# Reordering the head, the middle and the second token group of a fused attention and Mish-MLP kernel

## The chip, the cores and the metric

The kernel runs on one core of a Trainium2 chip. The metric is device time in microseconds (us), taken as the median of the runs shown; less is better.

## The reference

Four batches of eight heads with 768 tokens of 64 channels go through a causal attention whose scores decay with distance by a factor `lam` of each head and which has no softmax. It is computed block by block with a running state. The result, 3072 tokens of 512 channels, goes through an MLP.

```python
for b in range(S // 64):                       # blocks of 64 tokens
    intra = einsum('bhic,bhjc->bhij', qb, kb) * Dmask          # Dmask = lam ** (i - j), i >= j
    out[:, :, sl] = einsum('bhij,bhjd->bhid', intra, vb) + einsum('bhid,bhde->bhie', qb * lam_pow, kv_state)
    kv_state = lam_block * kv_state + einsum('bhsd,bhse->bhde', kb * rev_pow, vb)
x = out.transpose(0, 2, 1, 3).reshape(3072, 512)
h = x @ w_in                                   # 512 x 2048
out = (h * tanh(softplus(h))) @ w_out          # 2048 x 512
```

The matrix products run in fp16 with sums in fp32.

## The kernel before

**Tiling.** The kernel works with chunks of 128 tokens. Each of the six *groups* n = 0 to 5 holds the n-th chunk of all four batches, so 512 tokens; chunk i is group i // 4 and batch i % 4. For each group there are three kinds of work: attention, which fills `xt[n]` (the MLP's input, transposed); mm1, 16 *units* of 128 hidden columns with four matmuls of 512 tokens each into one PSUM bank `ph`, after which ScalarE writes Mish of it into `hsg`; and mm2, the product with w_out. Group 0 does mm2 plainly (`mm2_unit`, L542: 16 steps of four matmuls into a bank `po`, batches 0 and 1 first, then 2 and 3). Groups 1 to 5 do it by Strassen-like products of quarters (`fast_unit`, L685: seven steps of two blocks of eight 256-column matmuls), which need sums of weights (`weight_sum`, L559) and of tokens (`token_sum`, L572) from VectorE, named `tsum` and `gsum`.

**Order.** The schedule is written by hand: every engine executes its instructions in the order of the program. The main loop (L737) lists the units of group n and, after given units (`room`, L754 and L756), puts in *pieces* of the attention of group n + 1. PSUM has eight banks: `ph` twice, `po` twice, and `pk`, `pq`, `pS` and `pO` once each. An instruction that takes a bank waits until the reader of what was there is done.

**The head (L700 to L736).** GpSimd (POOL) issues the loads of chunks 1 to 3 of group 0, then w_in in six transfers (its first quarter in three), w_out in four, then group 1's chunks. Chunk 0's k and q come over two other queues. Without a state yet, the attention of chunk c is `first_t` (L211: PE transposes k and q into `pk` and `pq`, ScalarE and VectorE copy them out as `pkT` and `pqT`), `first_s` (L228: scores in two banks, `pS` and one `po`, and two VectorE products with the decay mask `dm`, giving `sb`) and `first_o` (L241: the product with v into `pO`, copied by ScalarE into `xt[0]`). The order on PE is t0 s0 t1 s1 o0 t2 s2 o1 t3 o2 s3, units 0 and 1 on the first 384 tokens around o3, and then mm1. `busy(m)` (L161) puts m matmuls of 512 zero columns in between. `pair_decays` (L188, two small VectorE copies and an exponential on ScalarE) stands between s0 and t1, and the exponential for `lk` and the load of the Mish table between s0 and o0.

**Group 0 to group 1.** After units 2 to 9 the kernel builds the states of group 0 in eight halves (`att_kv`, L296; `att_w`, L310). Group 1's attention is done in eight *halves* (one chunk, four heads): `att_a` (L324: transposes, the state product `pv`; on VectorE `qT` and two sums `raw`, on ScalarE two copies `kz`), `att_s` (L355: scores; VectorE's `sb`) and `att_o` (L367: output; ScalarE's `xt`). 21 of these 24 pieces stand between mm2 steps 8 to 15, and the last three between the first units of group 1.

**Group 1 and on.** The attention of group n + 1 for n of 1 and more comes as six pieces for two pairs of chunks: `pair_a` (L389: state products; VectorE's four `raw` and one `state`), `pair_s` (L408: scores and the state's part; VectorE's four `sb`), `pair_o` (L438: output; VectorE's four `xtok`, then two DMA transposes into `xt`). In group 1 they stand after units 6, 8, 10, 11, 14 and 18, counted over 16 mm1 units and 14 blocks of the fast product, and after units 2, 5, 7, 9, 12 and 16 later. `turn` (L268) scales k on VectorE or GpSimd and issues two DMA transposes on SyncE's queue (SP).

Of the kernel before, what the change touches and what calls it, by code (L numbers as in the profile page):

```python
# [20 lines left out]
def kernel(  # L21
# [12 lines left out]
    C = 128  # L34
# [49 lines left out]
    cuts = (0, 128, 256, DF // WS)  # L84
    win0 = [const.tile([128, NKC, b_ - a_], F16, name=f"win0{a_}") for a_, b_ in zip(cuts, cuts[1:])]
    win = [None] + [const.tile([128, NKC, DF // WS], F16, name=f"win{s}") for s in range(1, WS)]
    wout = [const.tile([128, NKI // WS, DMO], F16, name=f"wout{s}") for s in range(WS)]

    def load_win(s):
        w = DF // WS  # L90
        if s == 0:
            for t, a_, b_ in zip(win0, cuts, cuts[1:]):
                nc.gpsimd.dma_start(
                    out=t, in_=moe_w_in[:, a_:b_].rearrange("(k p) f -> p k f", p=128))
            return
# [61 lines left out]
    nc.vector.tensor_scalar(out=ident, in0=rel, scalar1=0.0, scalar2=None, op0=ALU.is_equal)  # L157
# [3 lines left out]
    def busy(m):  # L161

        t = ps.tile([128, 4 * C], F32, name="busy", tag="ph", bufs=2)
        for _ in range(m):
            nc.tensor.matmul(t, kzero, kzero2, start=True, stop=True)  # L165
# [13 lines left out]
    lbc = const.tile([128, JP], F32, name="lbc")  # L179
    lqt = const.tile([128, H], F32, name="lqt")  # L180

    def decays(t):
        for j in range(JP):
# [4 lines left out]
    def pair_decays():  # L188
        lnh = lnb.rearrange("p (j t) -> p j t", t=2)
        for hp in range(2):  # L190
            rs = slice(64 * hp, 64 * hp + 64)
            nc.vector.tensor_copy(lnp[rs, :], lnh[rs, :, hp])
        nc.scalar.activation(lbc, lnp, AF.Exp, scale=float(C))
# [6 lines left out]


    lbm = const.tile([128, JP, 128], F32, name="lbm")
# [8 lines left out]
    def first_t(c):  # L211

        out_ = []
        for src, name in ((k0 if c == 0 else kn[c], "pk"), (q0 if c == 0 else qn[c], "pq")):
# [7 lines left out]
            if name == "pk":  # L222
                nc.scalar.activation(out_[-1], pt, AF.Copy)
            else:
                nc.vector.tensor_copy(out_[-1], pt)
# [50 lines left out]
    wst = [[const.tile([128, 2, 128], F16, name=f"w{b}{hf}") for hf in range(2)] for b in range(B)]  # L276
# [33 lines left out]
    def att_w(s):  # L310
        n, b, hf = s.n, s.b, s.hf
        w = wst[b][hf]
        lb = lbm[:, 2 * hf : 2 * hf + 2, :]
        if n == 0:
            nc.vector.tensor_tensor(out=w, in0=s.pv, in1=lb, op=ALU.mult)
        else:
            sum_rows(n, b, s.pv, 2 * hf, 2, lambda rs: w[rs, :, rs])
# [6 lines left out]
    def att_a(s):  # L324
# [25 lines left out]
        elif hf == 0:  # L350
            turn(i + 1)
# [15 lines left out]
    def att_o(s):  # L367
# [7 lines left out]
        for p in range(2):  # L375
            j = 2 * hf + p
            nc.tensor.matmul(psO[:, p, :], wst[b][hf][:, p, :], s.qT[:, p, :],
# [101 lines left out]
    def att_pieces(n):  # L479
        halves = att_halves(n)  # L480
        out_ = []
        for t in range(len(halves) + 2):
            if t < len(halves):
                out_.append((att_a, halves[t]))
            if 0 <= t - 1 < len(halves):
                out_.append((att_s, halves[t - 1]))
            if 0 <= t - 2 < len(halves):
                out_.append((att_o, halves[t - 2]))
        return out_


# [10 lines left out]
    def mm1_part(n, ni, lo, hi):  # L502

        if lo == 0:
            ph_t[ni] = ps.tile([128, GT], F32, name="ph", tag="po" if ni == 2 and n < 2 else "ph", bufs=2)
        w = DF // WS // 128
        for kc in range(NKC):
            nc.tensor.matmul(  # L508
                ph_t[ni][:, lo:hi],
                win0[min(ni, 2)][:, kc, max(ni - 2, 0) * 128 : max(ni - 2, 0) * 128 + 128] if ni < w  # L510
                else win[ni // w][:, kc, (ni % w) * 128 : (ni % w) * 128 + 128],
# [3 lines left out]
    def mm1_unit(n, ni):  # L515
# [7 lines left out]
        mark.append(hsg[n][0:1, ni, 0:1])  # L523

# [175 lines left out]
    first_halves = att_halves(0)  # L700
    nh = len(first_halves)
# [12 lines left out]
    first_t(1)  # L714
    nc.scalar.preload_act_table(AF.Mish)
    busy(1)
    first_s(1)
    first_o(0)
    busy(3)
    first_t(2)  # L720
    busy(1)
    first_s(2)
    first_o(1)
    busy(3)
    first_t(3)
    first_o(2)
    busy(1)
    first_s(3)
    mm1_part(0, 0, 0, GT - C)
    first_o(3)  # L730
    mm1_part(0, 1, 0, GT - C)
    scale_k(0)
    nc.vector.memset(lbm, 0.0)
# [3 lines left out]
    for n in range(NG):  # L737
        units = [(mm1_unit, (n, ni)) for ni in range(NKI)]

        if n == 0:  # L740
# [114 lines left out]
```

## Time and profile before

| | |
|---|---|
| median of three runs | 206.41 us (206.38, 206.41, 208.25) |
| time of the profiled execution | 206.31 us |
| its span, first to last instruction | 204.5 us |
| PE busy | 195.3 us |
| VectorE busy | 137.8 us |
| ScalarE busy | 90.3 us |
| GpSimd busy | 82.8 us |

The 1.8 us between span and time lie around the instructions. PE's busy time holds the zero matmuls of `busy`, and a matmul's end is modelled, so busy PE is not PE at full pace. How much each stage loses is read from the chain of work and from the pace of unbroken matmuls. In the rows, PEld is the weight load of PE, DVE is VectorE, ACT is ScalarE, and L with a number is the line of the kernel.

### The profile page before, as it was taken

The numbers are of one execution on the slowest core, as the hardware profiler recorded it, in microseconds if no ns is written. First come the engines' busy times: TensorE is split into PE (matmuls) and PEld (weight loads), VectorE is DVE, ScalarE is ACT, GpSimd is POOL, SyncE is SP. The second block draws the span as 40 slices with busy tenths as digits, with TensorE's granted clock in tenths as the row PEclk, the third lists the DMA queues.
The fourth block names the chain that finished last, engine by engine and source line by source line (L and its number), as shares of the span: only waits on it lengthen the run. The fifth ranks groups of instructions, "written<-read, shape, count | busy, mean of one in ns | idle before, by whom it ended". The sixth has DMA issues, their size and how long they took to land.

```text
span 204.5 us, 4393 instructions
## 1 busy us (share of the span) xinstructions
PE 195.3 (95%) x1736; PEld 127.3 (62%) x1736; DVE 137.8 (67%) x277; ACT 90.3 (44%) x159; POOL 82.8 (40%) x128
## 2 busy tenths in 40 slices
PE   7788999999999979999999999999999999999993
PEld 2455544467655459855578855488745688544893
DVE  5857670689879996759994759995727774122543
ACT  5375668466674522045542065431156530466310
POOL 7997333899903876000898000996000000000000
PEclk9999999999999999999999999999999999999999
DMA  9999999999999999974699993999983122300014
GB/s 131 140 149 182 206 207 198 154 212 152 157 181 154 89 132 121 204 201 82 45 122 168 229 187 77 79 126 180 173 221 67 39 55 84 123 0 3 2 67 138
DMA packets 112471, 26.77 MB, mean 131 GB/s; under 512 B 102594, under 2 KB 111938, under 8 KB 112450
## 3 DMA queue, kind: packets, MB, share of 16 engines
q0 software_dynamic: 78080, 13.37, 91.8%
q1 hardware_dynamic: 31392, 10.49, 26.6%
q10 hardware_dynamic: 2978, 2.62, 4.5%
q8 instruction: 13, 0.21, 0.5%
q14 instruction: 8, 0.07, 0.1%
HBM read 27.26 MB, written 6.29 MB: 164 GB/s over the span
## 4 chain that ended last, share of the span: by engine, by line
PE 82%; DVE 9%; ACT 3%; DMA 2%; issue 1%; ACTq 0%; DVEq 0%
PE ph L508 36%; PE z L614 13%; PE x L614 9%; PE y L614 7%; PE po L531 6%; DVE raw L287 2%; DMA qn<-in_q_dram 2%; PE fin L614 2%; PE pS L419 2%; PE pO L446 2%; DVE sb L435 2%; DVE gsum L587 1%; PE pv L397 1%; PE pS L360 1%; PE pv L303 1%
## 5 line engine op out<-in xcount | busy, mean ns | idle before, releaser
L508 PE MATMUL ph<-xt,win 128*128 128x512 f16 (+2 forms) x404 | 88.7, 369 | 0.4 <-ACT hsg L522 0.2
L522 ACT ACTIVATE hsg<-ph 128x512 f16<-128x512 f32 x96 | 57.0, 597 | 66.7 <-PE ph L508 66.6
L508 PEld LDWEIGHTS <-win 128*128 128x128 f16 x404 | 37.0, 98 | 37.6 <-issue 0.6
L614 PEld LDWEIGHTS <-gsum 128*128 128x128 f16 x336 | 31.6, 98 | 3.5
L614 PEld LDWEIGHTS <-hsg 128*128 128x128 f16 x240 | 23.2, 98 | 4.4 <-issue 0.8
L498 POOL COPY paced<-hsg 1x1 f16<-1x1 f16 x27 | 7.6, 281 | 42.2 <-ACT hsg L522 42.2
L435 DVE TENSOR_TENSOR sb<-pS,maskT 128x512 f16<-128x512 f32 x32 | 19.9, 683 | 5.3 <-PE pS L419 5.2
L69 POOL DMA_DIRECT2D kn<-in_k_dram x23 | 20.6, 896 | 6.1 <-DMA wout<-in_moe_w_out_dram 1.7
L80 POOL DMA_DIRECT2D vz<-in_v_dram x24 | 21.1, 887 | 4.2 <-DMA win<-in_moe_w_in_dram 1.7
L77 POOL DMA_DIRECT2D qn<-in_q_dram x23 | 20.3, 884 | 5.5 <-DMA wout<-in_moe_w_out_dram 3.3
L587 DVE TENSOR_TENSOR gsum<-hsg 128x1024 f16<-128x1024 f16 x20 | 13.6, 685 | 10.9 <-ACT hsg L522 10.9
L614 PE MATMUL x<-wout,hsg 128*128 128x256 f16 x160 | 19.6, 273 | 0.5 <-DVE sb L435 0.5
L614 PE MATMUL z<-tsum,gsum 128*128 128x256 f16 x160 | 19.3, 273 | 0.0
L264 DVE TENSOR_TENSOR ktil<-kn,lk 128x512 f16<-128x512 f16 (+1 forms) x20 | 13.6, 686 | 6.8 <-DMA kn<-in_k_dram 6.6
L531 PE MATMUL po<-wout,hsg 128*128 128x512 f16 x64 | 15.1, 379 | 0.0
L287 DVE TENSOR_TENSOR raw<-pv,state 64x256 f32<-64x256 f32 x24 | 10.1, 420 | 6.0 <-PE pv L397 5.7
L454 DVE TENSOR_TENSOR xtok<-pO,lqt 128x256 f16<-128x256 f32 x32 | 11.3, 417 | 1.0 <-PE pO L446 0.9
L667 DVE TENSOR_TENSOR u<-z,p 128x512 f32<-128x512 f32 x5 | 3.5, 691 | 10.0 <-PE z L614 10.0
L531 PEld LDWEIGHTS <-hsg 128*128 128x128 f16 x64 | 6.0, 98 | 5.9
L614 PE MATMUL z<-tsum,hsg 128*128 128x256 f16 x80 | 9.6, 273 | 0.0
L587 DVE TENSOR_TENSOR gsum<-hsg,gsum 128x1024 f16<-128x1024 f16 x10 | 6.6, 688 | 3.8 <-PE z L614 3.8
L165 PE MATMUL busy<-kzero 128*128 128x512 f16 x18 | 7.6, 517 | 1.2 <-DVE kzero L150 1.2
(102 smaller groups left out, 213.2 us busy)
## 6 DMA issues: line engine op xcount, KB each, us to landing
out_dram<-osum SPq DMA_DIRECT2D x14, 256.0 KB, 2.4
vz<-in_v_dram POOLq DMA_DIRECT2D x24, 128.0 KB, 5.8
kn<-in_k_dram POOLq DMA_DIRECT2D x23, 128.0 KB, 5.2
qn<-in_q_dram POOLq DMA_DIRECT2D x23, 128.0 KB, 5.5
wout<-in_moe_w_out_dram POOLq DMA_DIRECT2D x4, 512.0 KB, 16.2
win<-in_moe_w_in_dram POOLq DMA_DIRECT2D x3, 512.0 KB, 9.9
out_dram<-osum ACTq DMA_DIRECT2D x5, 256.0 KB, 4.0
out_dram<-osb ACTq DMA_DIRECT2D x4, 256.0 KB, 6.3
```

The costliest lines, as they stand in the source:

```text
L69: nc.gpsimd.dma_start(out=kn[i], in_=chunk_rows(k, i))
L77: nc.gpsimd.dma_start(out=qn[i], in_=chunk_rows(q, i))
L80: nc.gpsimd.dma_start(out=vz[i % NVB][:, :, 0:D], in_=chunk_rows(v, i))
L264: (nc.gpsimd if B < i <= 2 * B else nc.vector).tensor_tensor(out=t, in0=kn[i], in1=bc(lk, 2, D), op=ALU.mult)
L287: nc.vector.tensor_tensor(out=raw[rs, b % 2, j0 : j0 + nj, :], in0=pv[rs, :, rs], in1=olds(rs), op=ALU.add)
L435: nc.vector.tensor_tensor(out=s.sb[m][t], in0=sc[m][t], in1=bc(maskT, 1, JP), op=ALU.mult)
L454: nc.vector.tensor_tensor(out=xtok[m][:, :, t, :], in0=s.pO[t][:, m], in1=bc(lt[:, :, t], 2, D), op=ALU.mult)
L508: nc.tensor.matmul(ph_t[ni][:, lo:hi], win0[min(ni, 2)][:, kc, max(ni - 2, 0) * 128 : max(ni - 2, 0) * 128 + 128] if ni < w else win[ni // ...
L522: nc.scalar.activation(hsg[n][:, ni, :], ph_t.pop(ni), AF.Mish)
L531: nc.tensor.matmul(po, hsg[n][:, ki, b * C : (b + 1) * C], wout[part][:, kk, :], start=(ki == 0), stop=(ki == NKI - 1),)
L587: nc.vector.tensor_tensor(out=gsum[n, i][:, ks, :], in0=a, in1=b, op=op)
L614: nc.tensor.matmul(t, lhs(kk, b), rhs(kk, c, c + w), start=(fresh and kk == 0 and (alone or i == 0)), stop=(kk == HK - 1), skip_group_chec ...
```

## The change

Four things change, all of them up to the end of group 1; groups 2 to 5 keep their order.

1. *Loads and head.* The first quarter of w_in is one transfer instead of three and goes behind v of chunk 1, ahead of the loads of chunks 2 and 3. The exponentials move ahead of the copy of k0, and the Mish table load to s0. `pair_decays` becomes four copies and goes between t1 and s1. The order on PE becomes t0 s0 t1 s1 o0 o1, units 0 to 3 on tokens 0 to 255, kv0 t2 s2 kv1 o2 t3, units 0 to 3 on tokens 256 to 383, s3 o3, units 0 to 3 on tokens 384 to 511, with `busy` in between. These four units are written as `mm1_duo`: two units share a bank, each with 256 tokens, and one Mish covers both. The states of group 0 are built by whole chunks (`first_kv`, `first_w`).
2. *mm2 of group 0* runs over four banks: parts 0 and 1 of all four batches, then parts 2 and 3 batch by batch. All eight weight sums stand among these steps.
3. *Attention of group 1.* 13 pieces stand after mm2 steps 10 to 15 and 11 after the first six duos of group 1.
4. *mm1 of group 1* is 16 duos: eight for tokens 0 to 255, then eight for tokens 256 to 511. The pieces of group 2's attention stand after units 12, 14, 15, 17, 19 and 22.

```diff
-    cuts = (0, 128, 256, DF // WS)
-    win0 = [const.tile([128, NKC, b_ - a_], F16, name=f"win0{a_}") for a_, b_ in zip(cuts, cuts[1:])]
-    win = [None] + [const.tile([128, NKC, DF // WS], F16, name=f"win{s}") for s in range(1, WS)]
+    win = [const.tile([128, NKC, DF // WS], F16, name=f"win{s}") for s in range(WS)]
...
-    for f, i in ((load_q, 1), (load_v, 0), (load_k, 2), (load_q, 2)):
-        f(i)
     nc.gpsimd.iota(ek, pattern=[[0, 1]], base=MID, channel_multiplier=-1,
                    allow_small_or_imprecise_dtypes=True)
-    for f, i in ((load_v, 1), (load_k, 3), (load_q, 3), (load_v, 2), (load_v, 3)):
+    for f, i in ((load_q, 1), (load_v, 0), (load_v, 1), (load_win, 0), (load_k, 2), (load_q, 2),
+                 (load_v, 2), (load_k, 3), (load_q, 3), (load_v, 3)):
         f(i)
-    for s in range(WS):
+    for s in range(1, WS):
         load_win(s)
...
     def pair_decays():
-        lnh = lnb.rearrange("p (j t) -> p j t", t=2)
-        for hp in range(2):
-            rs = slice(64 * hp, 64 * hp + 64)
-            nc.vector.tensor_copy(lnp[rs, :], lnh[rs, :, hp])
-        nc.scalar.activation(lbc, lnp, AF.Exp, scale=float(C))
+        for src, dst in ((lnb, lnp), (lbh, lbc)):
+            lnh = src.rearrange("p (j t) -> p j t", t=2)
+            for hp in range(2):
+                rs = slice(64 * hp, 64 * hp + 64)
+                nc.vector.tensor_copy(dst[rs, :], lnh[rs, :, hp])
...
+    def first_kv(c):
+
+        first_pv[c] = ps.tile([128, JP, 128], F32, name="pv", tag="po", bufs=2)
+        for j in range(JP):
+            nc.tensor.matmul(
+                first_pv[c][:, j, :].rearrange("p (a e) -> p a e", a=2),
+                ktil[c][:, 2 * j : 2 * j + 2, :].rearrange("p h c -> p (h c)"),
+                vz[c][:, 2 * j : 2 * j + 2, 0:D], start=True, stop=True,
+            )
+
+    def first_w(c):
+        nc.vector.tensor_tensor(out=wst[c], in0=first_pv[c], in1=lbm, op=ALU.mult)
...
+    def mm1_duo(n, g, lo, hi):
...
+        h = GT // 2
+        half = lo // h
+        w = DF // WS // 128
+        if (n, g, half) not in duo_t:
+            duo_t[n, g, half] = ps.tile([128, 2, h], F32, name="ph", tag="ph", bufs=2)
+        t = duo_t[n, g, half]
+        for m in range(2):
+            ni = 2 * g + m
+            for kc in range(NKC):
+                nc.tensor.matmul(
+                    t[:, m, lo - half * h : hi - half * h],
+                    win[ni // w][:, kc, (ni % w) * 128 : (ni % w) * 128 + 128],
+                    xt[n][:, kc, lo:hi], start=(kc == 0), stop=(kc == NKC - 1),
+                )
+        if hi == half * h + h:
+            nc.scalar.activation(hsg[n][:, 2 * g : 2 * g + 2, half * h : half * h + h], t, AF.Mish)
...
-            po_t[b] = ps.tile([128, DMO], F32, name="po", tag="po", bufs=2)
+            po_t[b] = ps.tile([128, DMO], F32, name="po", tag="po" if b < 2 else "ph", bufs=2)
...
+    nc.scalar.activation(lbh, lnb, AF.Exp, scale=float(C))
+    nc.scalar.activation(lk, lnb, AF.Exp, scale=ek)
     nc.scalar.activation(k0, kn[0], AF.Copy)
-    decays(0)
+    decays(0, range(JP))
+    decays(1, range(JP - 1))
     nc.vector.tensor_copy(q0, qn[0])
+    decays(1, range(JP - 1, JP))
     nc.scalar.activation(dm[:, 0], dm[:, 0], AF.Exp)
-    decays(1)
-    first_t(0)
+    busy(2, C)
+    first_t(0, between=4)
     nc.scalar.activation(dm[:, 1], dm[:, 1], AF.Exp)
+    nc.scalar.preload_act_table(AF.Mish)
     busy(1)
     first_s(0)
+    first_t(1)
     pair_decays()
-    nc.scalar.activation(lk, lnb, AF.Exp, scale=ek)
-    busy(2)
-    first_t(1)
-    nc.scalar.preload_act_table(AF.Mish)
-    busy(1)
+    busy(3)
     first_s(1)
...
     for hp in range(2):
         rs = slice(64 * hp, 64 * hp + 64)
         nc.vector.tensor_copy(lbm[rs, :, rs], bc(lbc[rs, :], 2, D))
...
+    first_o(0)
+    busy(4)
+    first_o(1)
+    scale_k(0)
+    scale_k(1)
+    mm1_duo(0, 0, 0, 2 * C)
+    mm1_duo(0, 1, 0, 2 * C)
+    first_kv(0)
+    first_t(2)
+    first_w(0)
+    busy(2, tag="pO")
+    first_s(2)
+    first_kv(1)
+    busy(3, tag="pO")
+    first_o(2)
+    first_t(3)
+    mm1_duo(0, 0, 2 * C, 3 * C)
+    mm1_duo(0, 1, 2 * C, 3 * C)
+    first_s(3)
+    first_w(1)
+    scale_k(2)
+    scale_k(3)
+    busy(4, tag="pO")
+    first_o(3)
+    mm1_duo(0, 0, 3 * C, 4 * C)
+    mm1_duo(0, 1, 3 * C, 4 * C)
...
+    pieces = [(step[w[0]], halves[int(w[1])]) for w in (
+        "a0 a1 s0 a2 s1 o0 a3 s2 o1 s3 o2 o3 a4 a5 s4 a6 s5 o4 s6 o5 a7 s7 o6 o7").split()]
+    room = {26: 1, 27: 2, 28: 3, 29: 3, 30: 2, 31: 2}
+    units = [(mm1_unit, (0, ni)) for ni in range(4, NKI)]
+    units += [(mm2_unit, (0, b, part)) for part in range(2) for b in range(B)]
+    units += [(mm2_unit, (0, b, part)) for b in range(B) for part in range(2, WS)]
+    for u, (fn, args) in enumerate(units, 4):
+        rest = fn(*args)
+        if u < 6:
+            first_kv(u - 2)
+            first_w(u - 2)
...
+        for i, s in {16: ((0, 0),), 18: ((0, 1),), 21: ((1, 0), (2, 0), (3, 0)),
+                     24: ((1, 1), (2, 1), (3, 1))}.get(u, ()):
+            weight_sum(i, s)
+        if u == 25:
+            scale_k(B)
+        attend(room.get(u, 0), "po")
+        if rest:
+            rest()
+
+    for n in range(1, NG):
+        if n == 1:
+            units = [(mm1_duo, (n, g, lo, lo + GT // 2)) for lo in (0, GT // 2) for g in range(NKI // 2)]
+            for u, m in enumerate((2, 3, 2, 1, 2, 1)):
+                fn, args = units.pop(0)
+                fn(*args)
+                attend(m, "po")
+                if u == 1:
+                    next_state(n, 0)
+                elif u == 5:
+                    next_state(n, 1)
+                if u > 2:
+                    turn((n + 1) * B + u - 3)
...
-            room = dict.fromkeys((6, 8, 10, 11, 14, 18) if n == 1 else (2, 5, 7, 9, 12, 16), 1)
+            pieces = chunk_pieces(n + 1)
+            room = dict.fromkeys((12, 14, 15, 17, 19, 22) if n == 1 else (2, 5, 7, 9, 12, 16), 1)
...
+        sums = {9: ((2, 0),), 10: ((2, 1),), NKI - 3: ((0, 0),), NKI - 2: ((1, 0),)}
+        if n == 1:
+            sums = {9: ((2, 0),), 11: ((2, 1),), NKI - 3: ((0, 0), (1, 0))}
+        sums.update({NKI - 1: ((0, 1), (1, 1)), NKI + 2: ((3, 0),), NKI + 3: ((3, 1),)})
+        for u, (fn, args) in enumerate(units, NKI + 14 - len(units)):
+            fn(*args)
...
+            for i, part in sums.get(u, ()):
+                token_sum(n, i, part)
+            if n == 1 and u == 8:
+                turn((n + 1) * B + 3)
...
+            attend(room.get(u, 0), "po" if u < NKI - 1 else "ph")
```

More of the change, by code (lines that the diff above doesn't have):

```diff
@@ L179, with decays @@
     lbc = const.tile([128, JP], F32, name="lbc")
+    lbh = const.tile([128, H], F32, name="lbh")
     lqt = const.tile([128, H], F32, name="lqt")
[L182 to L183 removed]
+    def decays(t, js):
+        for j in js:
             nc.vector.scalar_tensor_tensor(
@@ L222, in first_t @@
             if name == "pk":
+                if between:
+                    busy(between, C)
                 nc.scalar.activation(out_[-1], pt, AF.Copy)
@@ new lines, with attend @@
+    mm1_duo(0, 0, 0, 2 * C)
[19 more added lines that the diff above has]
+    mm1_duo(0, 1, 3 * C, 4 * C)
+    def attend(m, spare):
+        for _ in range(m):
+            f2, s = pieces.pop(0)
+            s.spare = spare
+            f2(s)
@@ new lines @@
+    for n in range(1, NG):
[11 more added lines that the diff above has]
+                    turn((n + 1) * B + u - 3)
+            while ahead:
+                ahead.pop(0)()
+        else:
+            units = [(mm1_unit, (n, ni)) for ni in range(NKI)]
+        units += [(fast_unit, (n, step, blk)) for step in range(7) for blk in range(2)]
@@ L773 @@
         times = range(8, 20)
-        for u, (fn, args) in enumerate(units):
-            rest = fn(*args)
+        sums = {9: ((2, 0),), 10: ((2, 1),), NKI - 3: ((0, 0),), NKI - 2: ((1, 0),)}
[4 more added lines that the diff above has]
+            fn(*args)
             if later and u in times:
```

153 lines of the change are left out of this document (31 added, 122 removed).

## The prediction

> **What bounds the kernel now.** I read the page's chain of work first, then the chain in order of time, then the time-ordered rows of the head, and last the groups of the stretch from 40.31 to 57.81 us.
>
> ```profile
> PE 82%; DVE 9%; ACT 3%; DMA 2%; issue 1%; ACTq 0%; DVEq 0%
> ```
>
> The chain runs through PE for 82% of the span. The pieces in order of time give PE's pace and show where others set it:
>
> ```profile
> 20.42 0.11 PE pv L303 x2
> ...
> 27.36 5.18 PE ph L508 x24
> 32.54 7.77 PE po L531 x36
> ...
> 57.81 3.61 PE ph L508 x16
> ...
> 61.68 0.42 DVE raw L287
> ...
> 63.46 0.69 DVE state L292
> 64.15 0.60 DVE tsum L568
> 64.79 2.48 DVE sb L435 x4
> 67.27 1.20 DVE gsum L587 x2
> ...
> 70.88 1.42 DVE xtok L454 x4
> ...
> 74.28 1.91 PE x L614 x16
> ...
> 80.15 1.75 PE z L614 x16
> ...
> 87.14 2.59 PE ph L508 x12
> ...
> 92.76 0.55 PE pS L419 x16
> 93.32 0.23 PE pO L427 x16
> ...
> 95.38 0.45 PE pv L397 x8
> ...
> 97.56 0.47 PE pO L446 x16
> ```
>
> A matmul costs 5.18/24 = 0.216 us with 512 columns, 1.75/16 = 0.109 with 256, 0.11/2 = 0.056 with 128. A unit or mm2 step is 4 x 0.216 = 0.863; a duo or fast block is 8 x 0.109 = 0.873. From 87.14 on PE never waits, and the change leaves those groups alone. So the new time is the old one plus the shift of the start of group 2's mm1, now at 87.14. What lies ahead of it splits at 32.54, where group 0's mm1 ends (call it M). From M to 87.14 are 54.6 us. The work in it: mm2 of group 0, 16 x 0.863 = 13.8; attention of group 1, 128 x 0.056 = 7.2; its mm1, 13.8; its fast product, 14 x 0.873 = 12.2; attention of group 2, 4 pair pieces of 0.45/2 per chunk = 0.9, 2 x (0.55 + 0.23) = 1.56 and 2 x 0.47 = 0.94, so 3.4. Sum 50.4: 4.2 us are lost, 1.7 of them up to 57.81 and 2.5 from there, where DVE carries the chain from 61.68 to 74.28.
>
> **The head.** These rows carry its chain:
>
> ```profile
> 7.10 0.61 PE L235 MATMUL pS<-pqT,pkT 64*128 64x128 f16 x8 [0.35 <-DVE pqT L225]
> ...
> 7.64 1.04 PE L165 MATMUL busy<-kzero 128*128 128x512 f16 x2
> ...
> 7.79 1.29 DVE L239 TENSOR_TENSOR sb<-pS,dm 128x512 f16<-128x512 f32 x2 [0.74 <-PE pS L235]
> ...
> 9.33 0.64 PE L165 MATMUL busy<-kzero 128*128 128x512 f16 x1
> ...
> 10.73 0.40 PE L235 MATMUL pS<-pqT,pkT 64*128 64x128 f16 x8 [0.77 <-ACT pkT L223]
> ...
> 11.16 1.29 DVE L239 TENSOR_TENSOR sb<-pS,dm 128x512 f16<-128x512 f32 x2 [0.94 <-PE pS L235]
> ...
> 12.81 0.42 DVE L225 COPY pqT<-pq 128x512 f16<-128x512 f16 x1 [0.36 <-PE pq L217]
> ...
> 17.71 0.55 PE L249 MATMUL pO<-sb,vz 128*128 128x128 f16 x7 [0.37 <-DVE sb L239]
> ...
> 18.30 0.60 ACT L251 ACTIVATE xt<-pO 128x512 f16<-128x512 f32 x1 [1.88 <-PE pO L249]
> ```
>
> ```profile
> L192 DVE COPY lnp<-lnb x2: 149/376/602, 9.0 to 9.2; 64x4 f32<-64x4 f32 x2
> ```
>
> Links: 0.43 from a score's start to its sb (10.73 to 11.16), 1.29 for two sb, 0.05 to the output matmuls, 0.59 to the copy xt (17.71 to 18.30), 0.60 for it, and as much for pkT, a copy of the same size. s0 stays at about 7.05: moving the exponentials ahead of k0's copy is free, since that copy waits for its load, and splitting the decays delays q0 as much as it hastens the mask. sb of chunk 0 ends at 9.05, pqT of chunk 1 at 9.45. PE does s0 (0.54, 7.10 to 7.64), t1 (eight quarter-width matmuls at the fillers' cold pace of 1.04 - 0.64 = 0.40 each, 0.8) and three fillers (1.2) until 9.6, so s1 starts 1.1 us earlier than at 10.73, where it waited for pkT. But `pair_decays` now lies between pqT and sb of chunk 1 on DVE, with four copies instead of two. The pair took 149 and 602 ns; four give 0.6 if all are like the first, 2.4 if all are like the second; I take twice the pair, 1.5, the nearest row. sb of chunk 1 then runs from 10.95 to 12.24, o1 starts at 12.29, xt of chunk 1 is done at 12.29 + 0.59 + 0.60 = 13.48.
>
> The Trainium skill, page "SBUF — State Buffer", section "Who interferes with whom", says that a VectorE copy in a two-port mode and GpSimd lock each other out for a whole instruction. The trace agrees as far as GpSimd issues a load beside both copies and one took four times the other. If each copy met that lock the sum would end 0.9 us later, if none did 0.9 earlier.
>
> Is w_in there by then? These rows bound it:
>
> ```profile
> L80 POOL DMA_DIRECT2D vz<-in_v_dram x1: 883/883/883, 3.5 to 3.5; - x1
> DMA to landing us min/median/max: 4.2/4.2/4.2
> ```
>
> ```profile
> L103 POOL DMA_DIRECT2D wout<-in_moe_w_out_dram x4: 837/849/864, 15.0 to 17.2; - x4
> DMA to landing us min/median/max: 13.4/16.2/18.9
> ```
>
> A chunk load is issued each 0.9 us and lands 4.2 later; four 512 KB weights land from 28.4 to 36.1, so 2.57 apart. v of chunk 1, one place behind this v of chunk 0, is issued at about 4.6 and lands at 8.8, w_in's quarter behind it at about 11.4, then k2, q2, v2, k3, q3, v3 each 0.9 later: q2 at 13.2, q3 at 15.9, v3 at 16.8. None is waited for below. On POOL the head issues two transfers fewer, so all later loads come a little sooner; no price.
>
> Duos of units 0 and 1, 2 and 3 on 256 tokens: 13.53 to 15.28. kv0 0.22, t2 at 15.50. ACT has two Mish ahead of pkT, so pkT ends at 16.63 and s2 starts at 16.68. On DVE `first_w` (an sb in size, 0.69) stands ahead of sb: sb of chunk 2 from 17.26 to 18.55, o2 at 18.60, xt at 19.79. t3 comes only after o2, so chunk 3 doesn't overlap chunk 2: duos on the third chunk 19.85 to 20.75, s3 20.75, sb 21.18 to 22.47, o3 22.52, xt 23.71, duos on the last chunk 23.76 to 24.66. Unit 4 needs a bank that Mish leaves at 25.0. Twelve units and kv2, kv3 are left: 12 x 0.863 + 0.45 = 10.8. M = 35.8 against 32.54: **+3.3**. Before, a chunk went through in some 2.6 us (scores at 10.73, 13.30, 15.94) because t of the next stood ahead of o. The bounds: the copies give -0.9 to +0.9, and 0.6 the other way if pkT and `first_w` overlap better than I set them; so +1.8 to +4.3.
>
> **mm2 and group 1's attention.**
>
> ```profile
> L347 ACT ACTIVATE kz<-pk 64x256 f16<-64x256 f32 x16 | 6.0, 377 | 4.0 <-PE pk L336 3.4 <-PE pv L303 0.4
> L364 DVE TENSOR_TENSOR sb<-pS,maskT 128x512 f16<-128x512 f32 x8 | 5.5, 692 | 1.0 <-PE pS L360 0.8
> L287 DVE TENSOR_TENSOR raw<-pv,w 64x128 f32<-64x128 f32 x16 | 4.5, 283 | 0.1
> ...
> L344 DVE TENSOR_TENSOR qT<-pq,lq 128x256 f16<-128x256 f16 x8 | 3.4, 422 | 1.4 <-PE pq L339 0.7 <-PE pv L303 0.2
> ...
> L384 ACT ACTIVATE xt<-pO 128x256 f16<-128x256 f32 x8 | 3.1, 383 | 2.3 <-PE pO L381 2.2
> ...
> L522 ACT ACTIVATE hsg<-ph 128x512 f16<-128x512 f32 x2 | 1.1, 594 | 0.5 <-PE ph L508 0.5
> ```
>
> mm2 runs without waits for 11 steps (the weights land before 36.1), to M + 9.5, and the weight sums lie under it. Then the halves come. With T the start of a0, PE has a0 (0.34), an mm2 step, a1, s0 (0.22), a step and a2 until T + 3.0; DVE must do qT (0.42), two raw (0.57) and sb0 (0.69) after a1's transposes at T + 1.4, with 0.35 until it can start: sb0 ends at T + 3.45, and s1 waits 0.5 for its bank. Followed so through the pieces, PE waits again for sb2 ahead of s3 (0.4), for xt of o3 ahead of the first duo (0.3), for kz5, now queued behind a Mish, ahead of a6 (0.5), and for sb5 and kz7 ahead of s6 and s7 (0.45 each): 2.6, with 0.1 given back by slack in between, 2.5. ACT has two kz, one xt and one Mish per half, 1.73 us, as much as PE's 16 x 0.056 + 0.873 = 1.77. Eight duos of tokens 0 to 255 are done at M + 9.5 + 5 x 0.863 + 7.2 + 8 x 0.873 + 2.5 = M + 30.5. Loss 2.5 against 1.7: **+0.8**, bounds 0 (as before) to +1.7 (twice it).
>
> **The rest of group 1.** Call M + 30.5 zero. `pair_a` stands after five more duos and ends at 4.8; its sums follow gsum and start at 5.0 on DVE. From there DVE's order is raw 1.78, state 0.69, two gsum 1.2, sb 2.48, two gsum 1.2, raw 1.78, state 0.69, xtok 1.42: the second `pair_s` can write pO at 16.3. PE's work to that place is 12 x 0.873 + 0.45 + 0.78 + 0.45 + 0.47 + 0.55 = 13.2, so it waits 3.1. Then DVE does two gsum and four sb, to 20.1, PE needs 2.9, waits 0.9, ends `pair_o` at 20.3 and the last seven blocks at 26.5. Loss 3.9 against 2.5: **+1.4**. The tsum that moved (three sums and the 0.60 at 64.15) came before this chain or lay in it once, so it saves little; `pair_a` comes four units later beside DVE than it did. Bounds: 0 to +2.4, another wait of 1 us. Last, xt of group 2:
>
> ```profile
> L456 SPq DMA_TRANSPOSE xt<-xtok x2: 1190/1239/1288, 79.8 to 81.1; - x2
> DMA to landing us min/median/max: 4.3/4.3/4.4
> ```
>
> The last xtok is written at 21.9, the second transpose issued at 22.45 and landed at 26.75: **+0.25**, bounds 0 and +1.2 if SP is late by one transpose. The turn's DMAs moved on SP come before it.
>
> **Sum.** 3.3 + 0.8 + 1.4 + 0.25 = 5.75; the profiled execution's 206.31 (span 204.5 and 1.8 around it, 0.1 below the median 206.41) gives 212.1.
>
> **Rivals.** (a) *The second half loses no more than now*: only the head counts, 206.3 + 3.3 = 209.6. For it: the moved weight sums free DVE; against it: DVE has its chain later than before. (b) *The halves of mm1 fill every wait* from the first piece to group 2, the other side: -4.2 + 3.3, 205.4. It decides against "slower" once the loss from M on is under 4.2 - 3.3 + 2.1 = 3.0. Against it: pO's release hangs on 11.3 us of DVE work in a row, and PE has 13.2 - 4.8 = 8.4 between. (c) *The clock*: the fillers at 7.64 and 9.33 took 0.40 a step, twice the later 0.216. If PE dropped to that pace once between 13 and 24, where it now waits often, a window of 3.4 us would cost up to 1.7, 213.8. The trace speaks against it: from 10.73 on no row is at the slow pace in spite of waits of 0.77. The Trainium skill, page "TensorE: Matmul & The Clock Gate", section "What's actually happening", has the clock halved after an idle window of about 3.4 us; by that rule, too, waits under a microsecond don't reach it.
>
> **How the numbers follow.** The forecast has 0.55, (a) 0.20, (b) 0.10, (c) 0.07; 0.08 is left for a mechanism on the fast side that I don't see, the chain of chunks 2 and 3 being shorter. The sums of the bounds are 1.8 and 9.6 (208.1 and 215.9); leaving the far end of the second out, 208.0 to 214.5 holds the forecast, (a) and (c). One per cent, 2.1 us, is what a measurement tells from no change: faster 0.08, same 0.12 ((b) and the low edge of (a)), slower 0.80.
>
> **What would show it.** In the changed kernel's trace: the first mm1 matmul near 13.5; scores of chunks 2 and 3 some 4 us apart; mm2 starting near 35.8; PE's second wait for xtok of about 3 us; group 2's mm1 near 93. Wrong is the forecast if mm2 starts before 33.5, or if the time from there to group 2's mm1 stays under 55.

## The result and the profile after

The changed kernel takes 212.72 us (median of four runs, 212.69 to 213.47). The kernel before, on the same chip, takes 207.13 us (206.38 to 208.25). The ratio is 1.027, with a 95% interval of 1.021 to 1.034: slower, by about 5.6 us. The profiled execution is the 213.47 one, with a span of 211.7 us; the other three have spans of 210.9 to 211.0.

The chain in order of time answers to the one shown of before (start, length, engine, what, line, how often):

```profile
10.70 1.30 DVE sb L233 x2
...
13.28 1.91 PE ph L529 x16
...
35.65 9.50 PE po L544 x44
...
64.18 6.11 PE ph L529 x56
...
82.22 0.41 PE pO L430 x15
82.62 3.38 PE x L627 x16
86.01 1.01 PE z L627 x8
...
93.60 2.59 PE ph L498 x12
```

Group 0's mm2 starts at 35.65 instead of 32.54, and group 2's mm1 at 93.60 instead of 87.14. So the head costs 3.1 us, the stretch from mm2 to group 2 costs 93.60 - 35.65 - 54.6 = 3.35, and another 0.7 (211.7 - 204.5 - 6.46) is lost later. Of that, the PE row at 158.93 further down shows a wait for a transposed key. The other three spans are 0.7 to 0.8 shorter, so that wait is probably one of the profiled execution alone.

The row at 82.62 is new in kind: 16 matmuls of 256 columns take 3.38 us where the same form took 1.75 before. The windows show why. Their columns are the window, its length, the busy time of PE, weight load, DVE, ACT and POOL with instruction counts, the granted clock, and the DMA share and rate:

```profile
80.00:82.00 2.00, 0.50 (x8) 0.32 (x8) 1.95 (x5) 0.02 (x1) 1.58 (x3) 1.00 1.52 97
...
83.00:84.00 1.00, 1.00 (x7) 0.72 (x5) 1.00 (x3) 0.00 (x0) 0.00 (x0) 0.50 1.68 157
...
85.00:86.00 1.00, 1.00 (x6) 0.71 (x5) 0.76 (x2) 0.00 (x0) 0.00 (x0) 0.50 0.52 43
```

PE counts as fully busy from 83 to 86, but the granted clock is 0.50: busy is not the same as fast. Right before it PE had waited, as the time-ordered rows of PE show (the bracket holds the idle time and what ended it):

```profile
74.94 0.38 PE L400 MATMUL pv<-vz,ktil 128*128 128x128 f16 x4 [0.46 <-ACT hsg L535]
...
79.31 0.45 PE L422 MATMUL pS<-qraw,kraw 64*128 64x128 f16 x9
80.04 0.39 PE L422 MATMUL pS<-qraw,kraw 64*128 64x128 f16 x7 [0.28 <-DVE raw L281]
...
81.89 0.73 PE L430 MATMUL pO<-state,qraw 64*128 64x64 f16 x16 [1.45 <-DVE xtok L457]
...
158.93 0.40 PE L422 MATMUL pS<-qraw,kraw 64*128 64x128 f16 x8 [0.52 <-DMA kraw<-ktil]
```

A bracket counts from the modelled end of the row before, so it is shorter than the stretch without matmuls. The row at 79.31 holds nine matmuls of 0.55/16 = 0.034 us, 0.31 in all, and the next starts at 80.04: that is 0.42 and not 0.28. Counted so, the wait ahead of 81.89 is 1.61.

In the head, the first weight load of mm1 waited for w_in until 13.05, and the first matmul for xt of chunk 1, whose copy ended at 13.23; so the two ended 0.2 us apart. The first two fences have these rows (PEld is the weight load), the others the issues of v of chunks 0 and 1, w_in's quarter and q of chunk 3 on POOL, with the time from issue to landing:

```profile
13.28 1.91 PE L529 MATMUL ph<-xt,win 128*128 128x256 f16 x16 [0.69 <-ACT xt L245]
```

```profile
13.05 1.85 PEld L529 LDWEIGHTS <-win 128*128 128x128 f16 x16 [0.63 <-DMA win<-in_moe_w_in_dram]
```

```profile
L80 POOL DMA_DIRECT2D vz<-in_v_dram x2: 883/890/896, 3.6 to 4.5; - x2
DMA to landing us min/median/max: 4.3/4.4/4.4
```

```profile
L89 POOL DMA_DIRECT2D win<-in_moe_w_in_dram x1: 782/782/782, 5.3 to 5.3; - x1
DMA to landing us min/median/max: 7.7/7.7/7.7
```

```profile
L77 POOL DMA_DIRECT2D qn<-in_q_dram x1: 947/947/947, 9.5 to 9.5; - x1
DMA to landing us min/median/max: 7.7/7.7/7.7
```

v of chunk 1 lands at 4.5 + 4.4 = 8.9 and w_in at 5.3 + 7.7 = 13.0, so the 512 KB cost 4.1 us of the queue, and the loads behind them land 7.7 us after their issue instead of 4.2 to 4.4. The four copies of `pair_decays` on VectorE and the scores of chunks 2 and 3 on PE, to which the prediction gave times, stand in the time-ordered rows of the two engines:

```profile
9.16 0.62 DVE L188 COPY lnp<-lnb 64x4 f32<-64x4 f32 x2
9.79 0.88 DVE L188 COPY lbc<-lbh 64x4 f32<-64x4 f32 x2
```

```profile
16.39 0.40 PE L229 MATMUL pS<-pqT,pkT 64*128 64x128 f16 x8
...
20.39 0.40 PE L229 MATMUL pS<-pqT,pkT 64*128 64x128 f16 x8
```

Both are near what was forecast, 1.5 us together and 4.0 apart.

### The profile page after: what moved, and what is told of

Same layout as the page of the kernel before. It is cut to its first block, busy times and chain, and to the rows that moved or that the text cites. A ratio compares the mean times of both kernels' runs of the same rounds, so it can differ in the third digit from the quotient of the medians.

```text
span 211.7 us, 4550 instructions
## 1 busy us (share of the span) xinstructions
PE 199.4 (94%) x1823; PEld 136.4 (64%) x1823; DVE 137.7 (65%) x275; ACT 89.9 (42%) x159; POOL 81.0 (38%) x126
## 3 DMA queue, kind: packets, MB, share of 16 engines
q0 software_dynamic: 77024, 13.37, 93.5%
## 4 chain that ended last, share of the span: by engine, by line
PE 81%; DVE 10%; ACT 3%; DMA 3%; issue 1%; ACTq 0%; DVEq 0%
PE ph L498 29%; PE z L627 12%; PE x L627 8%; PE ph L529 7%; PE y L627 7%; PE po L544 6%; DMA kraw<-ktil 3%; PE pS L422 2%; PE fin L627 2%; DVE sb L233 2%; PE pO L449 2%; DVE raw L281 1%; DVE sb L438 1%; PE pv L400 1%; PE busy L159 1%
## 5 line engine op out<-in xcount | busy, mean ns | idle before, releaser
L498 PE MATMUL ph<-xt,win 128*128 128x512 f16 x304 | 68.9, 379 | 0.2 <-ACT hsg L535 0.2
L498 PEld LDWEIGHTS <-win 128*128 128x128 f16 x304 | 28.8, 98 | 31.9 <-issue 0.4
L627 PEld LDWEIGHTS <-hsg 128*128 128x128 f16 x240 | 23.9, 101 | 4.2
L600 DVE TENSOR_TENSOR gsum<-hsg 128x1024 f16<-128x1024 f16 x20 | 13.7, 687 | 14.6 <-ACT hsg L511 10.9
L627 PE MATMUL x<-wout,hsg 128*128 128x256 f16 x160 | 21.1, 286 | 0.0
L529 PE MATMUL ph<-xt,win 128*128 128x256 f16 (+1 forms) x176 | 19.5, 263 | 1.6 <-ACT xt L245 1.6
L529 PEld LDWEIGHTS <-win 128*128 128x128 f16 x176 | 15.6, 98 | 3.5 <-issue 1.2
L544 PEld LDWEIGHTS <-hsg 128*128 128x128 f16 x64 | 6.1, 98 | 6.4
L349 DVE TENSOR_TENSOR qT<-pq,lq 128x256 f16<-128x256 f16 x8 | 3.4, 423 | 10.0 <-PE pv L297 6.6
## 6 DMA issues: line engine op xcount, KB each, us to landing
wout<-in_moe_w_out_dram POOLq DMA_DIRECT2D x4, 512.0 KB, 16.3
```

Of the source, the lines that this page charges most:

```text
L498: nc.tensor.matmul(ph_t[ni][:, lo:hi], win[ni // w][:, kc, (ni % w) * 128 : (ni % w) * 128 + 128], xt[n][:, kc, lo:hi], start=(kc == 0), s ...
L529: nc.tensor.matmul(t[:, m, lo - half * h : hi - half * h], win[ni // w][:, kc, (ni % w) * 128 : (ni % w) * 128 + 128], xt[n][:, kc, lo:hi] ...
L544: nc.tensor.matmul(po, hsg[n][:, ki, b * C : (b + 1) * C], wout[part][:, kk, :], start=(ki == 0), stop=(ki == NKI - 1),)
L600: nc.vector.tensor_tensor(out=gsum[n, i][:, ks, :], in0=a, in1=b, op=op)
L627: nc.tensor.matmul(t, lhs(kk, b), rhs(kk, c, c + w), start=(fresh and kk == 0 and (alone or i == 0)), stop=(kk == HK - 1), skip_group_chec ...
```

## Experiments

Theory A, after the result: three losses of separate cause. (1) In the head, w_in's early transfer and the chain that takes chunks 2 and 3 one after the other: 3.1. (2) From mm2 on, the later and longer VectorE chain: 2.0. (3) A fall of the clock behind the wait at 81.89: 1.3. The main rivals: the head's loss is given back later (or the rest's loss hangs on the head), and the clock is only a by-product that moves nothing.

**The old head before the new rest.**

```diff
-    for f, i in ((load_q, 1), (load_v, 0), (load_v, 1), (load_win, 0), (load_k, 2), (load_q, 2),
-                 (load_v, 2), (load_k, 3), (load_q, 3), (load_v, 3)):
+    for f, i in ((load_q, 1), (load_v, 0), (load_k, 2), (load_q, 2), (load_v, 1), (load_k, 3),
+                 (load_q, 3), (load_v, 2), (load_v, 3)):
...
-    units = [(mm1_unit, (0, ni)) for ni in range(4, NKI)]
+    units = [(mm1_unit, (0, ni)) for ni in range(NKI)]
```

(With it, the head's statements and `pair_decays` as before, and `first_kv` after units 2, 4, 6 and 8.)

> The changed kernel with the loads and the head of the kernel before (w_in's quarter in three pieces behind chunk 3, units 0 and 1 on 384 tokens, whole units from there), group 0's states by chunk, and everything from mm2 on as changed. My theory: mm2 starts near 32.6 us as before instead of 35.65, and all that follows keeps its shape, so the time falls by the head's 3.1 us from 212.7 to about 209.6. Rival: the later stages wait for VectorE and transfers and not for PE, so an earlier start only makes their waits longer: 211.5 to 212.7.

210.18 us (209.33 to 210.46), ratio to the kernel before 1.014 [1.009, 1.019]. Its chain and time-ordered rows:

```profile
34.43 9.50 PE po L558 x44
...
91.06 2.59 PE ph L512 x12
```

```profile
12.16 1.49 PE L167 MATMUL busy<-kzero 128*128 128x512 f16 x3
...
80.61 0.73 PE L438 MATMUL pO<-state,qraw 64*128 64x64 f16 x16 [1.45 <-DVE xtok L465]
```

From mm2 to group 2 it takes 56.63: the new rest costs 2.0 with the old head, too. The clock stayed at 1.00 here in spite of the same wait of 1.45. That mm2 starts at 34.43 and not near 32.6 is a miss: three fillers at 12.16 took 1.49, where the kernel before had them at 0.81 at 11.52. PE came to its full pace only at about 15.5 in this execution; more of that below.

**The new head before the old rest** (the changed kernel's loads and head, then units, halves and pairs in the order of the kernel before).

```diff
-        units = [(mm1_unit, (n, ni)) for ni in range(NKI)]
+        units = [(mm1_unit, (n, ni)) for ni in range(4 if n == 0 else 0, NKI)]
```

> The other way round: the loads, the head and the states by chunk as changed, everything from mm2 on as in the kernel before (two banks for mm2, whole units in group 1, old pieces and rooms). My theory: mm2 starts near 35.6 instead of 32.54, the 54.6 us from there to group 2 stay, the clock stays at 1.0: about 209.5. Rival: the head's loss is an effect of running it with the changed middle, and the old middle makes it good again: 206.5 to 208.

209.98 us (209.42 to 212.08), ratio 1.014 [1.008, 1.020].

```profile
35.76 7.77 PE po L559 x36
...
90.36 2.59 PE ph L513 x12
```

mm2 starts 3.2 late and group 2 follows 54.6 later, to the tenth as before. So the head's loss is carried through in full, and with the run above the two parts add: 3.1 + 2.0, and the clock.

**Only the loads in the new order** (kernel before).

```diff
-    for f, i in ((load_q, 1), (load_v, 0), (load_k, 2), (load_q, 2)):
...
+    for f, i in ((load_q, 1), (load_v, 0), (load_v, 1), (load_win, 0), (load_k, 2), (load_q, 2),
+                 (load_v, 2), (load_k, 3), (load_q, 3), (load_v, 3)):
```

> The kernel before with nothing changed but the loads: w_in's first quarter as one transfer behind v of chunk 1, and the small iota ahead, as in the change. By the prediction's estimate of the landings (q2 at 13.2, q3 at 15.9) t2 would wait 1.0 us and t3 1.2: mm2 at about 33.7, 207.5. By the landings that the changed kernel shows (w_in at 13.0, q2 at 14.7, q3 at 17.2) t2 waits 2.4 and t3 2.5: mm2 near 35, 208.8. Rival: hidden, 206.5.

209.50 us (208.46 to 210.45), ratio 1.010 [1.004, 1.016].

```profile
6.97 7.63 DMA qn<-in_q_dram
...
34.80 7.77 PE po L522 x36
```

Moving w_in ahead of the chunks costs the old head 2.3 us at mm2 by itself: q of chunk 2, issued at 6.97, lands at 14.6, and the old head waits for it. The new head takes up chunk 2 later, at 15.25, and its PE waits for none of the chunk loads behind w_in.

**Chunk 3's transposes and scores ahead of chunk 2's output** (changed kernel).

```diff
     first_kv(1)
-    busy(3, tag="pO")
-    first_o(2)
     first_t(3)
-    mm1_duo(0, 0, 2 * C, 3 * C)
-    mm1_duo(0, 1, 2 * C, 3 * C)
+    busy(1, tag="pO")
+    first_o(2)
     first_s(3)
     first_w(1)
+    mm1_duo(0, 0, 2 * C, 3 * C)
+    mm1_duo(0, 1, 2 * C, 3 * C)
...
-    busy(4, tag="pO")
     first_o(3)
```

> The changed kernel with t3 ahead of o2 and s3 directly behind o2, as in the kernel before, the duos of the third chunk behind s3, and four fillers fewer. My theory: the head's cost is the serial chain of chunks 2 and 3; now sb of chunk 3 starts about 1.9 us earlier, mm2 starts near 33.8, time about 210.8. Rival: the loads of chunk 3, now behind w_in's quarter (q3 landed at 17.2, v3 at 18.1), or the duos themselves set the end of the head: mm2 stays near 35.5, 212.5.

210.74 us (209.72 to 210.97), ratio 1.016 [1.012, 1.021].

```profile
33.72 9.50 PE po L544 x44
...
80.66 2.96 PE x L627 x16
...
91.63 2.59 PE ph L498 x12
```

mm2 starts 1.93 earlier. So 1.9 of the head's 3.1 is the order t3 behind o2, although the loads stay late. The 2.3 of the run before belongs to the old head, which waits for the chunk loads, and is no part of the 3.1. The 1.2 that are left (33.72 against 32.54) no run takes apart. The clock fell here too (2.96 for the 16 matmuls), and from mm2 to group 2 it takes 57.9, as in the changed kernel.

**`pair_decays` behind the scores of chunk 1** (changed kernel).

```diff
-    pair_decays()
     busy(3)
     first_s(1)
+    pair_decays()
```

> The changed kernel with the four small copies behind s1, so behind the two sb of chunk 1 on VectorE instead of ahead of them. If the copies set the chain, as the prediction says, sb of chunk 1 ends 1.0 to 1.3 us earlier and the first duo would start at 12.0 to 12.3; but w_in's quarter landed at 13.0, so the duo starts near 13.1 instead of 13.28 and the time falls by 0.2 only: 212.5. If w_in isn't what holds it, 211.5.

211.66 us (211.11 to 212.66), ratio 1.021 [1.016, 1.026].

```profile
12.94 1.92 PE ph L529 x16
...
35.33 9.50 PE po L544 x44
...
91.95 2.59 PE ph L498 x12
```

With the 1.5 us of copies out of the way the first duo starts only 0.3 earlier, at the landing of w_in (12.9). Copies and transfer end at nearly the same time; either alone would hold it. The profiles of the five other kernels that keep the copies ahead of s1 say the same: the copies took 1.10 to 1.73 us there, and the first duo started at 13.08 to 13.37. Where they were fastest, in the run of the fillers further down, PE waited for w_in alone:

```profile
13.28 1.92 PE L529 MATMUL ph<-xt,win 128*128 128x256 f16 x16 [1.56 <-DMA win<-in_moe_w_in_dram]
```

The profiled execution of the late copies has the clock at 1.00, and 56.62 from mm2 to group 2.

**Eight fillers on PE ahead of group 1's second pair scores** (changed kernel; no wait is taken away, PE is kept busy).

```diff
+            if n == 1 and u == 19:
+                busy(8, tag="pS")
             attend(room.get(u, 0), "po" if u < NKI - 1 else "ph")
```

> The changed kernel with eight zero matmuls of 512 columns into the free bank pS ahead of the second pair_s of group 1, where PE waits from 80 to 82 us; no useful work moves. My theory: the wait of some 1.7 us is what halves the granted clock from 82.6 to 86.1; with fillers it stays at 1.0, 16 matmuls of 256 columns take 1.75 instead of 3.38, half a microsecond of it is lost again to the sb of the pair, and the time falls by 1.0 to 1.3 to about 211.5. Rival: the clock falls for another reason (the stretch from 74 on with its many short waits, or the pause in VectorE's chain itself) and the run still shows 0.5 there, with the time at 212.7 or above.

212.50 us (211.48 to 213.91), ratio 1.028 [1.021, 1.035]: the median does not move.

```profile
35.66 9.50 PE po L544 x44
...
92.28 2.59 PE ph L498 x12
```

In the profiled execution the clock is 1.00 throughout and group 2 starts 1.3 earlier, although PE does 1.7 us of work for nothing. But of four runs two had a mean clock of 0.992 again (213.4 and 213.9 against 211.5 and 211.6). The price of the fall is shown, that the fillers prevent it is not.

**The pairs as early as before.**

```diff
-            room = dict.fromkeys((12, 14, 15, 17, 19, 22) if n == 1 else (2, 5, 7, 9, 12, 16), 1)
+            room = dict.fromkeys((8, 10, 12, 13, 16, 20) if n == 1 else (2, 5, 7, 9, 12, 16), 1)
```

> The changed kernel with the pieces of group 2's attention after units 8, 10, 12, 13, 16 and 20 of group 1 instead of 12, 14, 15, 17, 19 and 22. My theory: VectorE's chain of 11.3 us starts 3.5 us earlier, into time in which VectorE idles, PE's second wait shrinks from some 2 to about 1.8 us at most, the clock stays up, and group 2 starts near 90.5 instead of 93.6: 209.5 to 210. Rival: VectorE has the same work in the same order, so the wait only moves; 212 to 213.

210.65 us (209.28 to 211.54), ratio 1.016 [1.010, 1.023]. This gains 2.1 in the median. The profile, in which group 2 starts at 92.24 and not near 90.5, has the clock's fall in it. So has, by its mean clock of 0.989, the run at 211.54; the two at 0.998 took 209.28 and 209.90, about the 209.5 to 210 that the theory forecast with the clock up. A row of PE and a window of two microseconds behind it:

```profile
77.93 0.72 PE L430 MATMUL pO<-state,qraw 64*128 64x64 f16 x16 [1.54 <-DVE xtok L457]
```

```profile
80.00:82.00 2.00, 2.00 (x11) 1.44 (x10) 1.93 (x4) 0.27 (x1) 1.32 (x4) 0.50 1.97 137
```

The longest wait, for xtok, moves with the pairs (1.54 instead of 1.45) and so does the fall of the clock: VectorE's chain sets it. But from mm2 (35.51) to group 2 it takes 56.73 with a fall, and in the changed kernel 57.95, also with one. So by these two profiles the place of the pairs counts, too: some 1.2 of the loss goes with the earlier place.

**All weight sums of group 1 in group 0** (kernel before).

```diff
-            if n == 0 and 19 <= u < 23:
-                weight_sum(0 if u < 21 else 2, u % 2)
-            if n == 1 and 4 <= u < 8:
-                weight_sum(1 if u < 6 else 3, u % 2)
+            if n == 0:
+                for i, s in {16: ((0, 0),), 17: ((0, 1),), 19: ((1, 0), (2, 0), (3, 0)),
+                             21: ((1, 1), (2, 1), (3, 1))}.get(u, ()):
+                    weight_sum(i, s)
```

> The kernel before with nothing changed but the weight sums: all eight among the mm2 steps of group 0 (after steps 16, 17, 19 and 21). My theory: the 0.60 us of tsum inside VectorE's chain of group 1 (64.15) falls away and the wait of PE near 72 shrinks by as much: 0.6 less, about 206.0. Rival: nothing, since the chain restarts later from other work: 206.6, no difference to be seen.

210.11 us (207.79 to 211.61), ratio 1.012 [1.006, 1.019]. Three of the six runs, at a mean clock of 0.984 to 0.992, took 211.35 to 211.61; the three at 1.00 took 207.79 to 208.86, where the kernel before had a median of 206.98. No gain is to be seen; how much of the loss is the clock's, six runs don't tell.

```profile
34.36 7.77 PE po L531 x36
...
88.57 2.59 PE ph L508 x12
```

The stretch from mm2 to group 2 is 54.2, only 0.4 shorter. The head again was at the slow pace (34.36).

**Is the head's pace what separates the runs of the kernel before?** Beside the runs of the loads, the new head, the moved sums and the late copies, five of its eleven were near 206.5 and five at 208.0 to 208.3. Two kernels have the changed kernel's early fillers in the head of the kernel before, the second also the moved weight sums:

```diff
+    busy(2, C)
-    first_t(0)
+    first_t(0, between=4)
```

> The kernel before, with fillers on PE in its first wait (two of 128 columns ahead of the transposes of chunk 0, four between k's and q's), as the changed kernel has them; nothing else. Theory: the kernel before takes 206.5 or 208.2 us because PE reaches its full pace in the head either at about 10.7 us or only at 15.5 (a 512-column filler 0.22 or 0.43 us), which the first fillers decide. Then PE is at full pace by 8.5 here (fillers of 512 columns 0.22 from the second chunk's transposes on), group 0's mm2 starts at 32.0 to 32.6 in the profile, and every run takes 206.0 to 206.7, where the kernel before has runs above 207.5 on the same chip. Rival 1: the two levels come from elsewhere (the clock later, or transfers); then this kernel has runs near 208 as often as the kernel before. Rival 2: the earlier pace delays nothing but the fillers push the scores back; then mm2 starts after 32.8.

> The kernel before with the same early fillers and with all weight sums of group 1 in group 0 (as in the run of the weight sums alone, whose head was at the slow pace until 15.5 us). If the head's pace was what hid the 0.4 us that the moved sums gave between mm2's start and group 2, this kernel takes 205.6 to 206.3 in all runs and group 2's mm1 starts 54.2 us after mm2. If the moved sums set off a fall of the clock by themselves, some runs stay at 208 or above, and the profile or the clock of those runs shows it behind 32 us.

The fillers alone: 207.58 us (206.39 to 208.88, 12 runs), ratio 1.001 [0.998, 1.005], with runs at both levels as the kernel before has. The idea that the first fillers decide falls. With the sums: 209.39 us (208.19 to 210.78), ratio 1.010 [1.006, 1.013]. The two profiles are worth more than the times, because the head's instructions on PE are the same in both. The fillers alone, the same three fillers and the start of mm2 (time-ordered rows, which begin some 0.16 before the chain's: 32.37 for the 32.54 of the kernel before):

```profile
11.00 0.81 PE L165 MATMUL busy<-kzero 128*128 128x512 f16 x3
...
32.42 7.93 PE L533 MATMUL po<-wout,hsg 128*128 128x512 f16 x36
```

And with the sums, the same two rows, and what happens on VectorE later:

```profile
12.21 1.49 PE L165 MATMUL busy<-kzero 128*128 128x512 f16 x3
...
34.15 7.93 PE L533 MATMUL po<-wout,hsg 128*128 128x512 f16 x36
```

```profile
37.91 0.69 DVE L266 TENSOR_TENSOR ktil<-kn,lk 128x512 f16<-128x512 f16 x1 [4.25 <-DMA kn<-in_k_dram]
...
40.93 2.38 DVE L570 TENSOR_TENSOR tsum<-wout,wout 128x1024 f16<-128x1024 f16 x1
43.23 1.52 DVE L570 TENSOR_TENSOR tsum<-wout,tsum 128x1024 f16<-128x1024 f16 x1
```

Same head, two paces: mm2 starts at 32.42 or at 34.15. That 1.7 us fits the distance of the two levels, but no run of the kernel before at 208 has a trace, so for these runs it stays argued. With the sums, group 2 starts at 90.06 in these rows, 55.9 after mm2 and not 54.2: VectorE stands 4.25 us for the key of chunk 4 with sums queued behind it, and two of these then take 2.38 and 1.52 instead of 0.68, beside loads and a `ktil` on GpSimd. The first half's qT comes late. In this execution moving the sums opens a new wait; in the one of the moved sums alone it saved 0.4.

**t3 early and the fillers together** (changed kernel, both edits above).

> The changed kernel with chunk 3's transposes and scores ahead of chunk 2's output (1.9 us of the head) and with eight fillers on PE ahead of group 1's second pair scores (1.3 us by the profile of that edit). If the two losses are in different places and add, 212.7 - 1.9 - 1.3 = 209.5, with mm2 at 33.7 and group 2's mm1 at 90.4. If the shorter head only moves the wait (for the state sums on VectorE) or the clock falls somewhere else, 210.5 to 211, with group 2 near 91.5.

209.79 us (209.60 to 209.84), ratio 1.011 [1.007, 1.016].

```profile
34.01 9.50 PE po L544 x44
...
90.66 2.59 PE ph L498 x12
```

mm2 to group 2's mm1 takes 56.65; all four runs have a clock of 1.00. The two losses are in different places and add. That the fillers kept the clock up is not shown, since it fell in two of the four runs with the fillers alone. What is left, some 3 us above the fastest runs of the kernel before, is 1.5 of the head (34.01 against 32.54) and the 2.0 from mm2 on. None of the eleven kernels is faster than the kernel before.

## Why the prediction was right, and where its steps were not

The time (212.1, range 208.0 to 214.5, against 212.72) and the sign are right, and the split at M holds: the head and the rest lose separately. Part of the agreement is luck: the sum did not hold the clock's 1.3, and without it the four terms come to 5.1 and not to 5.75. One argument in the head was wrong. The range's upper end, 214.5, does not follow from the bounds given, whose sum is 215.9, and 215.0 without the 0.9 between the second term and its far end.

- **The head, +3.3.** Measured 3.1 (M at 35.65 against 35.8) and 3.2 with the old rest behind it. *The copies* took 0.62 + 0.88 = 1.5 us as taken, in other profiles 1.10 to 1.73 (two of them 0.17 each, the others 0.44 and 0.68; whether these two met the lock that the Trainium skill, page "SBUF — State Buffer", section "Who interferes with whom", names, no run here separates); sb of chunk 1 ran from 10.70 to 12.00 against 10.95 to 12.24. *w_in* failed: the prediction had it land at 11.4 and the loads behind it 0.9 apart from there, and said none is waited for. It landed at 13.0. PE's weight load waited for it, and in other profiles the first duo itself; the loads behind it came some 1.5 late (q of chunk 2 at 14.7, q of chunk 3 at 17.2), but the new head needs these only at 15.25 and 18.55. The step that failed was taking 2.57 us, the spacing of four large transfers among themselves, for one that runs between small chunk loads; it cost 4.1. The first duo, 13.28 against 13.53, came where the chain of the copies had it; that the transfer ended 0.2 us before and not after is luck. *Chunks 2 and 3* were right: scores at 16.39 and 20.39, exactly the 4 us forecast, and turning the order back gives 1.9.
- **mm2 and group 1's attention, +0.8.** The first piece starts at M + 9.5 as forecast, and the last duo of the first half ends at 64.18 + 2 x 0.873 = 65.93, M + 30.3 against M + 30.5. So +0.6.
- **The rest of group 1, +1.4.** The second `pair_s` writes pO at 82.22, 16.29 us after zero; 16.3 was forecast from VectorE's order alone. With the 13.2 of work that the prediction added up, PE loses the 3.1 that it forecast, but in pieces. Counted from the starts of the rows and the pace, 3.0 of it are 0.63 ahead of 74.94 (four matmuls of pv start at 74.09), 0.42 ahead of 80.04, 1.61 ahead of 81.89 and 0.32 between the first matmul of pO and the rest. The wait of 0.9 ahead of `pair_o` was mis-sized: where the clock stays up, its first eight matmuls hardly wait and the other eight do, as in the run with the late copies (PE, time-ordered):

```profile
84.83 0.41 PE L449 MATMUL pO<-vz,sb 128*128 128x64 f16 x8
85.42 0.41 PE L449 MATMUL pO<-vz,sb 128*128 128x64 f16 x8 [0.19 <-DVE sb L438]
```

  With 0.47/16 = 0.029 us a matmul the wait is 85.42 - 84.83 - 8 x 0.029 = 0.36. The end of `pair_o` is met all the same: 85.83 in that run, whose zero is 65.55, so 20.28 against 20.3. In the profiled execution of the changed kernel the slow PE covers this wait.
- **xt of group 2, +0.25.** No wait for it is seen. Without the clock the two terms and this one come to 56.6 - 54.6 = 2.0 (four profiles: 56.63, 56.62, 56.62 and 56.65) against 2.45.
- **The clock, rival (c), 0.07.** Its price was right and its place wrong. A fall was priced at up to 1.7 us for 3.4 us at half pace, and placed between 13 and 24, where none came. At 82.6 it cost 1.63 + 0.14 on the rows, and 1.3 at group 2's start (57.95 against 56.62), since part of it stood in for the wait at `pair_o`. The prediction had a wait of 3.1 us in its own working at this place and did not hold that against the clock. The Trainium skill, page "TensorE: Matmul & The Clock Gate", section "What's actually happening", puts the fall behind an idle window of about 3.4 us. The trace differs: there is no single wait above 1.61 us, and from 80 to 82 PE was busy for 0.5 us.
- **Rival (a), only the head, 209.6,** is excluded by the old head before the new rest: 56.6 from mm2 on, not 54.6. **Rival (b)**, that the halves fill every wait, fails at the place the prediction named, pO's release.

Left open: why the clock falls in one execution and not in another with the same waits (a bracket of 1.45 with a fall in the changed kernel; without one in two other profiles), and the wait for a transposed key at 158.93.

## What to carry to other kernels

Before a large transfer is put ahead of small ones on a queue, price it by what it does to every load behind it, and by a row from the same place in the queue: here 512 KB cost 4.1 us between chunk loads and not the 2.57 seen among weights. Split the shift of the end at a point where the stages meet and test each side with the other one's old version; here 3.2 and 2.0 came back separately to a tenth. Where a working predicts waits of a microsecond or more on PE close together, add the price of a few microseconds at half clock, and read the granted clock before calling a busy PE a full one.

## What the runs showed of the hardware that was not expected

- PE's clock was granted at 0.50 for about 3.4 us after PE had been partly idle (brackets of 0.28 and 1.45 us within 2 us), in some executions and not in others. The fall does not begin at the wait: in windows of 0.1 us it starts at 82.75, 81.23 and 79.58 (changed kernel, t3 early, pairs early), so 0.9, 1.3 and 1.65 us after the wait for xtok has ended, with PE busy again, and it lasts about 3.4 us each time. Runs of one kernel with a mean clock of 1.00 and of 0.992 mostly lie 1 to 2 us apart (209.7 against 210.7 to 211.0 with t3 early), though not always: the fastest run of the old head before the new rest was at 0.992.
- The time at which PE first reaches full pace differs between executions of the same head: about 7.2 us in one, 14.5 in another, worth 1.7 us at mm2. The granted clock was given as 1.00 for both; only the length of the fillers shows it (0.81 or 1.49 for three). The Trainium skill, page "TensorE: Matmul & The Clock Gate", section "What's actually happening", says that the window which decides is free-running and does not restart with the kernel. The two profiles fit that, but the spread is more than the half microsecond it names.
- A load of 128 KB behind the 512 KB took 7.7 us from issue to landing, as did the chunk loads that followed in the head, against 4.2 to 4.4 ahead of it.
